# Six feed-forward slots take the quotient from a VectorE reciprocal in place of ScalarE's squared reciprocal root and a refining step

## The chip, the core and the metric

The kernel runs on one core of a Trainium2 chip. The core has five engines with queues of their own: TensorE (PE; its weight loads are PEld), VectorE (DVE), ScalarE (ACT), GpSimd (POOL) and SyncE (SP, which issues all transfers here). Each engine takes its instructions in the order in which they stand in its queue, and waits on semaphores for the others. The metric is the device time of one execution in microseconds: 607.78 us, the median of three runs (607.64 to 608.12).

## The reference

A retention layer is followed by a feed-forward layer with a rational activation. The change lies in the activation, the lines of P, Q and g.

```python
def _attn_ref(q, k, v):                      # B, H, S, D = 4, 8, 768, 64
    for t in range(S):
        state = gamma * state + einsum('bhd,bhe->bhde', k[:, :, t], v[:, :, t])
        y[:, :, t] = scale * einsum('bhd,bhde->bhe', q[:, :, t], state)
    return y

def _moe_ref(x, w_in, w_out, a, b):          # 3072 tokens, 512 -> 2048 -> 512
    h = x @ w_in
    P = a[0] + a[1] * h + a[2] * h * h + a[3] * h * h * h
    Q = 1.0 + abs(b[0]) * abs(h) + abs(b[1]) * h * h
    g = P / (Q + 1e-06)
    return g @ w_out
```

## The kernel before

The 3072 tokens are six blocks of 512, the 2048 hidden columns sixteen tiles of 128. One block with one tile is a slot: 96 of them, numbered by k in the order in which they run. The first two blocks share the first 32 slots by halves; then block 2 has slots 32 to 47, block 3 slots 48 to 63, and so on. Slots 40 to 42 are thus tiles 8 to 10 of block 2, slots 60 to 62 tiles 12 to 14 of block 3. While a block's slots run, the attention work for the next block is put between them.

A slot consists of an input product on TensorE (twelve matmuls at L734, into one of two PSUM banks that the slots use in turn, the tile `ph`), an elementwise chain on a 128x512 tile, and an output product (twelve matmuls at L753, into `po`). TensorE runs the input product of slot k, then the output product of slot k-2, and so on by turns. The input product of slot k+2 needs the bank of slot k, which is free when the last read of `ph` in slot k is over.

The chain of one slot, with the names of its steps:

| step | engine, line | what |
|---|---|---|
| A1 | ACT L796 | q = \|h\| |
| A2 | ACT L805 or POOL L801 | s = \|b0\| + \|b1\| q |
| A3 | ACT L811 | p = a2 + a3 h |
| P1 | POOL L816 | q = q s, so that q + 1 + 1e-6 is the denominator |
| D1 | DVE L824, L825 | p = (p h + a1) h, the numerator without a0 |
| A4 | ACT L831, L832 | s = reciprocal root of the denominator; ph = s squared |
| D2 | DVE L843, L844, L845 | q = denominator times ph; ph = (p + a0) ph; p = (2 - q) ph |
| A6 | ACT L851 | gh = p rounded to the matmul's type |
| P2 | POOL L855 | gl = p - gh |

L843 to L845 refine the estimate of the quotient by one step. The output product takes gh twice and gl once. The tiles p, q and s have two buffers each, gh and gl three.

What runs in which order is fixed beforehand: every step has a number, and the table ORDER lists these numbers; each engine's queue follows from it. In ScalarE's queue slot 40's A6 comes after slot 41's A1 and ahead of its A3 and A2; in the slots without attention work A6 of a slot comes behind A1, A3 and A2 of the next one and ahead of its A4. In VectorE's queue D2 of a slot stands ahead of D1 of the next. The tile qcon holds 1 + 1e-6, and par_sb the four coefficients a and both b. `aside` is false in every slot, as no entry of ENGINES moves that step.

Of the kernel before, what the change touches and what calls it, by code (L numbers as in the profile page):

```python
# [12 lines left out]
AF = mybir.ActivationFunctionType  # L13
ALU = mybir.AluOpType
# [8 lines left out]
class Buffer:  # L23


    def __init__(self, pool, options=None):
        self.pool, self.options, self.banks = pool, options, None
        self.users, self.end = 0, 0


class Step:
    def __init__(self, engines, cost, run, after, rank, takes, uses, tiled):
        self.engines, self.cost, self.run, self.rank = engines, cost, run, rank
        self.takes, self.uses, self.tiled = takes, [*takes, *uses], tiled
        self.after = [(a, 0) if isinstance(a, Step) else a for a in after if a]
        self.start = self.end = self.known = None
        self.waits = 0


class Plan:  # L40
# [7 lines left out]
    def step(  # L48
        self, engines, cost, run, after=(), rank=0.0, takes=(), uses=(), tiled=False, kind=None
    ):  # L50
        self.steps.append(Step(engines, cost, run, after, rank, list(takes), list(uses), tiled))
        return self.steps[-1]
# [12 lines left out]
def tile_retention_rational_ffn(  # L65
# [18 lines left out]
    nc = tc.nc  # L84
# [23 lines left out]
    par_sb = small[:, FEW - 6 : FEW]  # L108
    babs = small[:, FEW : FEW + 2]
    qcon = small[:, FEW + 2 : FEW + 3]  # L110
# [565 lines left out]
    def by(kind, key, default="ACT"):  # L676
        return (ENGINES.get((kind, key), default),)
# [92 lines left out]
    def slot(k, n, f, first, final):  # L770
        cell = {}
        ph = Buffer("psum", lambda: [["b0"], ["b1"]])
        p, q, s, gh, gl = (Buffer(x) for x in ("p", "q", "s", "gh", "gl"))
# [46 lines left out]
        aside = by("N", k, "DVE") == ("POOL",)  # L820
# [7 lines left out]

        def a4(_):
            s_ = cell["s"]  # L830
            nc.scalar.activation(s_, cell["q"], AF.Abs_reciprocal_sqrt, bias=qcon[:, 0:1])  # L831
            nc.scalar.activation(s_ if aside else cell["ph"], s_, AF.Square)  # L832

# [3 lines left out]

        def d2(_):
            p_, q_, ph_ = cell["p"], cell["q"], cell["ph"]
            if aside:  # L840
                nc.vector.scalar_tensor_tensor(ph_, ph_, par_sb[:, 0:1], cell["s"], ALU.add, ALU.mult)
            else:
                nc.vector.scalar_tensor_tensor(q_, q_, qcon[:, 0:1], ph_, ALU.add, ALU.mult)  # L843
                nc.vector.scalar_tensor_tensor(ph_, p_, par_sb[:, 0:1], ph_, ALU.add, ALU.mult)  # L844
            nc.vector.scalar_tensor_tensor(  # L845
                p_, q_, 2.0, ph_, ALU.subtract, ALU.mult, reverse0=True
            )
# [5 lines left out]
        def p2(_):  # L853
# [7 lines left out]
        D1 = step(("DVE",), (1440, 1440), d1, [A3], k, uses=[p, ph], kind="D1")  # L861
        A4 = step(
            ("ACT",), (1265, 1327), a4, [P1, None if aside else D1], k,
            uses=[q, s] if aside else [q, s, ph], kind="A4",
        )
        N1 = aside and step(("POOL",), (1350, 1400), n1, [A4], k, uses=[q, s], kind="N")
        D2 = step(
            ("DVE",), (1370, 1440) if aside else (2030, 2100), d2, [A4, D1, N1], k,
            uses=[p, q, ph, s] if aside else [p, q, ph], kind="D2",
        )  # L870
        A6 = turn("A6", step(("ACT",), (526, 610), a6, [D2], k, [gh], [p], kind="A6"))
        P2 = turn("P2", step(("POOL",), (1253, 1297), p2, [A6], k, [gl], [p, gh], kind="P2"))
# [67 lines left out]
    with tc.manual_schedule(  # L940
# [27 lines left out]
        for k, (n, f) in enumerate(order):  # L968
            while built < NSTEP and starts[built] <= k:
                gate = (gemms_in[k - 1], None) if k else None  # L970
                if built == B:
                    for b in range(0, B, 2):
                        first_states(b, STATES, None)
                many = 2 if built >= PAIRS else 1
                later_chunks(
                    built, many, RANKS.get(built, starts[built] + 0.5), LOADS.get(built, starts[built] / 100),
                    gate,
                )
                built += many
            a, b = turn_of(n, f)  # L980
            first, last = f == a, f + 1 == b
            if last and a:
                load_sums(n, gemms_out[-2])
            slot(k, n, f, first, last)
# [288 lines left out]
```

## Time and profile before

| | |
|---|---|
| median of three runs | 607.78 us |
| the profiled execution | 607.81 us, its span 606.0 us |
| TensorE busy | 98% of the span |
| VectorE busy | 74%, 672 instructions |
| ScalarE busy | 70%, 692 instructions |
| GpSimd busy | 56%, 290 instructions |
| matmuls of input and output product | 390 and 392 ns each in the trace, pipelined: twelve take 2.72 us |
| DVE L843 idle before | 112.1 us in total over 96 slots, 109.1 of it until ACT L832 |

The profile shows one execution. Its span goes from the first to the last instruction; the execution's own time is longer by what lies around the span. A group of instructions has its busy time, the mean duration of one in ns, and the idle time of the engine just ahead of them with what ended it. The timeline gives the start, the duration, the engine, the line and operation, and in brackets the engine's idle time before and what ended it. A duration includes the time until the result has landed, so the next instruction of an engine can begin a little before the end of the one ahead.

### The profile page before, as it was taken

The page shows a single profiled execution, that of the slowest core. Times are in us where ns is not written, and L with a number is a line of the kernel's source. Part 1 is how long each engine was busy: PE and PEld are TensorE (multiplying, and loading weights), DVE is VectorE, ACT ScalarE, POOL GpSimd, SP SyncE. Part 2 cuts the span into 40 slices and gives each one's busy share as a digit, 9 for nine tenths or more (in the row PEclk, how much of TensorE's full clock was granted, in tenths as well). Part 3 has the DMA queues.
Part 4 walks back from the last instruction along what each step waited for, and adds up shares of the span by engine and source line. Part 5 has one row for each costly group of instructions (what it writes and reads, how often), then busy time and mean ns, then how long its engine had stood idle before and what let it go on. Part 6 is the DMA issues. An engine that isn't in the chain of part 4 may idle for free.

```text
span 606.0 us, 12924 instructions
## 1 busy us (share of the span) xinstructions
PE 595.0 (98%) x5228; PEld 485.7 (80%) x5228; DVE 446.7 (74%) x672; ACT 425.7 (70%) x692; POOL 339.9 (56%) x290
## 2 busy tenths in 40 slices
PE   7989999999999999999999999999999999999997
PEld 5757888888888888878888888888888888888885
DVE  5899899998788778666677766567777666666663
ACT  2889799999756575756766765577675676777663
POOL 2789598888747454545435454454363445544452
PEclk9999999999999999999999999999999999999999
DMA  8989506013314253404005101400140000100001
GB/s 310 384 325 415 212 0 210 1 47 107 125 62 159 75 197 91 153 19 157 2 1 174 71 1 37 140 1 18 70 157 2 1 1 1 70 0 1 0 1 70
DMA packets 29980, 58.63 MB, mean 97 GB/s; under 512 B 3168, under 2 KB 8416, under 8 KB 29920
## 3 DMA queue, kind: packets, MB, share of 16 engines
q1 hardware_dynamic: 29920, 57.80, 27.0%
q8 instruction: 41, 0.67, 0.4%
q14 instruction: 19, 0.16, 0.1%
HBM read 49.40 MB, written 8.39 MB: 95 GB/s over the span
## 4 chain that ended last, share of the span: by engine, by line
PE 92%; DVE 1%; ACT 0%; issue 0%
PE po L753 44%; PE ph L734 42%; PE px L279 3%; PE pa L249 2%; PE pk L258 2%; PE po L150 0%; DVE t L706 0%; DVE px L316 0%; DVE u L703 0%; DVE mid L604 0%; DVE p L845 0%; DVE ph L844 0%; DVE state L663 0%; DVE q L843 0%; DVE after L613 0%; DVE p L824 0%
## 5 line engine op out<-in xcount | busy, mean ns | idle before, releaser
L816 POOL TENSOR_TENSOR q<-q,s 128x512 f32<-128x512 f32 x96 | 124.2, 1294 | 173.6 <-ACT s L805 164.2
L734 PE MATMUL ph<-xh,w 128*128 128x512 f32 (+2 forms) x776 | 208.1, 390 | 0.1
L753 PE MATMUL po<-w,gh 128*128 128x512 f32 x768 | 199.8, 392 | 0.0
L734 PEld LDWEIGHTS ph<-xh,w 128*128 128x128 f32 x776 | 143.8, 188 | 30.2 <-DVE p L845 0.5
L753 PEld LDWEIGHTS po<-w,gh 128*128 128x128 f32 x768 | 142.8, 188 | 30.8 <-ACT gh L851 0.3
L843 DVE SCALAR_TENSOR_TENSOR q<-q,small,ph 128x512 f32<-128x512 f32 x96 | 71.7, 747 | 112.1 <-ACT ph L832 109.1
L855 POOL TENSOR_TENSOR gl<-p,gh 128x512 fp32r<-128x512 f32 x96 | 124.3, 1295 | 38.9 <-ACT gh L851 21.9
L831 ACT ACTIVATE s<-q,small 128x512 f32<-128x512 f32 x96 | 69.6, 725 | 64.7 <-POOL q L816 64.7
L753 PE MATMUL po<-w,gl 128*128 128x512 f32 x384 | 110.4, 389 | 0.0
L796 ACT ACTIVATE q<-ph 128x512 f32<-128x512 f32 x96 | 57.3, 597 | 70.4 <-PE ph L734 69.9
L734 PE MATMUL ph<-xl,w 128*128 128x512 f32 (+2 forms) x388 | 103.2, 388 | 0.0
L734 PEld LDWEIGHTS ph<-xl,w 128*128 128x128 f32 x388 | 72.6, 188 | 15.2
L753 PEld LDWEIGHTS po<-w,gl 128*128 128x128 f32 x384 | 72.0, 188 | 15.4 <-POOL gl L855 0.4
L811 ACT ACTIVATE p<-ph,small 128x512 f32<-128x512 f32 x96 | 74.4, 775 | 0.0
L825 DVE SCALAR_TENSOR_TENSOR p<-p,small,ph 128x512 f32<-128x512 f32 x96 | 71.8, 748 | 3.4
L824 DVE TENSOR_TENSOR p<-ph,p 128x512 f32<-128x512 f32 x96 | 65.7, 684 | 8.8 <-ACT p L811 8.4
L844 DVE SCALAR_TENSOR_TENSOR ph<-p,small,ph 128x512 f32<-128x512 f32 x96 | 71.9, 749 | 0.0
L851 ACT CAST gh<-p 128x512 fp32r<-128x512 f32 x96 | 59.2, 616 | 13.2 <-DVE p L845 13.0
L845 DVE SCALAR_TENSOR_TENSOR p<-q,ph 128x512 f32<-128x512 f32 x96 | 65.9, 687 | 3.3
L832 ACT ACTIVATE ph<-s 128x512 f32<-128x512 f32 x96 | 57.8, 602 | 4.2 <-DVE p L825 0.8
L805 ACT ACTIVATE s<-q,small 128x512 f32<-128x512 f32 x73 | 59.3, 813 | 0.1
L715 POOL TENSOR_TENSOR w<-t,w 128x512 fp32r<-128x512 f32 x32 | 41.4, 1298 | 13.8 <-ACT w L712 13.3
(65 smaller groups left out, 429.3 us busy)
## 6 DMA issues: line engine op xcount, KB each, us to landing
v<-in_v SPq DMA_DIRECT2D x34, 256.0 KB, 5.2
raw<-in_w_in SPq DMA_DIRECT2D x16, 512.0 KB, 7.5
raw<-in_w_out SPq DMA_DIRECT2D x16, 512.0 KB, 7.5
qT<-in_qT SPq DMA_DIRECT2D x24, 256.0 KB, 4.6
kT<-in_kT SPq DMA_DIRECT2D x24, 256.0 KB, 4.4
k<-in_k SPq DMA_DIRECT2D x24, 256.0 KB, 4.7
out<-o SPq DMA_DIRECT2D x24, 256.0 KB, 2.4
q2T<-in_q2T SPq DMA_DIRECT2D x10, 256.0 KB, 5.7
```

Source lines behind the costliest of these rows:

```text
L734: nc.tensor.matmul(cell["ph"][:, t0:t1], w[0, f][:, part, kt * P : (kt + 1) * P], x[:, kt, t0:t1], start=(i == 0), stop=(i == 3 * NP - 1),)
L753: nc.tensor.matmul(o_tiles[n][tt], g_[:, tt * P : (tt + 1) * P], w[1, f][:, part], start=(first and m == 0), stop=(last and m == 2),)
L805: nc.scalar.activation(cell["s"], cell["q"], AF.Identity, bias=babs[:, 0:1], scale=babs[:, 1:2])
L811: nc.scalar.activation(cell["p"], cell["ph"], AF.Identity, bias=par_sb[:, 2:3], scale=par_sb[:, 3:4])
L816: nc.gpsimd.tensor_mul(cell["q"], cell["q"], cell["s"])
L824: nc.vector.tensor_mul(p_, ph_, p_)
L825: nc.vector.scalar_tensor_tensor(ph_ if aside else p_, p_, par_sb[:, 1:2], ph_, ALU.add, ALU.mult)
L831: nc.scalar.activation(s_, cell["q"], AF.Abs_reciprocal_sqrt, bias=qcon[:, 0:1])
L843: nc.vector.scalar_tensor_tensor(q_, q_, qcon[:, 0:1], ph_, ALU.add, ALU.mult)
L844: nc.vector.scalar_tensor_tensor(ph_, p_, par_sb[:, 0:1], ph_, ALU.add, ALU.mult)
L845: nc.vector.scalar_tensor_tensor(p_, q_, 2.0, ph_, ALU.subtract, ALU.mult, reverse0=True)
L855: nc.gpsimd.tensor_sub(cell["gl"], cell["p"], cell["gh"].bitcast(F32))
```

## The change

In slots 40, 41, 42, 60, 61 and 62, step A4 is one ScalarE pass that adds 1 + 1e-6 to q and leaves the denominator in s. Step D2 is VectorE's reciprocal of s into the bank `ph`, and one pass p = (p + a0) ph. There is no squaring, and no refining step. All other slots are as before, and ORDER is unchanged. That D2 names s among its tiles has no effect on the order, which is read from the table.

```diff
+DIVIDED = (40, 41, 42, 60, 61, 62)
...
         def a4(_):
             s_ = cell["s"]
+            if k in DIVIDED:
+                nc.scalar.activation(s_, cell["q"], AF.Identity, bias=qcon[:, 0:1])
+                return
             nc.scalar.activation(s_, cell["q"], AF.Abs_reciprocal_sqrt, bias=qcon[:, 0:1])
             nc.scalar.activation(s_ if aside else cell["ph"], s_, AF.Square)
...
         def d2(_):
             p_, q_, ph_ = cell["p"], cell["q"], cell["ph"]
+            if k in DIVIDED:
+                nc.vector.reciprocal(ph_, cell["s"])
+                nc.vector.scalar_tensor_tensor(p_, p_, par_sb[:, 0:1], ph_, ALU.add, ALU.mult)
+                return
             if aside:
...
         D2 = step(
             ("DVE",), (1370, 1440) if aside else (2030, 2100), d2, [A4, D1, N1], k,
-            uses=[p, q, ph, s] if aside else [p, q, ph], kind="D2",
+            uses=[p, q, ph, s], kind="D2",
         )
```

In the changed file the lines up to A4 are numbered 4 higher, those of the refining D2 11 higher. VectorE's queue from slot 40's D2 to slot 41's D2 before (xl and px belong to the attention work between them):

```order
L843 SCALAR_TENSOR_TENSOR q<-q,small,ph 128x512
L844 SCALAR_TENSOR_TENSOR ph<-p,small,ph 128x512
L845 SCALAR_TENSOR_TENSOR p<-q,ph 128x512
L331 TENSOR_TENSOR xl<-px,xh 128x2x2x128 x2
L824 TENSOR_TENSOR p<-ph,p 128x512
L825 SCALAR_TENSOR_TENSOR p<-p,small,ph 128x512
L843 SCALAR_TENSOR_TENSOR q<-q,small,ph 128x512
L844 SCALAR_TENSOR_TENSOR ph<-p,small,ph 128x512
L845 SCALAR_TENSOR_TENSOR p<-q,ph 128x512
```

And the same stretch of VectorE's queue in the changed kernel:

```order
L848 RECIPROCAL ph<-s 128x512
L849 SCALAR_TENSOR_TENSOR p<-p,small,ph 128x512
L335 TENSOR_TENSOR xl<-px,xh 128x2x2x128 x2
L828 TENSOR_TENSOR p<-ph,p 128x512
L829 SCALAR_TENSOR_TENSOR p<-p,small,ph 128x512
L848 RECIPROCAL ph<-s 128x512
L849 SCALAR_TENSOR_TENSOR p<-p,small,ph 128x512
```

Three passes of each slot have become two, and the others keep their places. ScalarE's queue from slot 40's A4 to slot 41's A4 before (xh is attention work):

```order
L831 ACTIVATE s<-q,small 128x512
L832 ACTIVATE ph<-s 128x512
L327 CAST xh<-px 128x2x2x128 x2
L796 ACTIVATE q<-ph 128x512
L851 CAST gh<-p 128x512
L811 ACTIVATE p<-ph,small 128x512
L805 ACTIVATE s<-q,small 128x512
L831 ACTIVATE s<-q,small 128x512
L832 ACTIVATE ph<-s 128x512
```

And in the changed kernel:

```order
L836 ACTIVATE s<-q,small 128x512
L331 CAST xh<-px 128x2x2x128 x2
L800 ACTIVATE q<-ph 128x512
L862 CAST gh<-p 128x512
L815 ACTIVATE p<-ph,small 128x512
L809 ACTIVATE s<-q,small 128x512
L836 ACTIVATE s<-q,small 128x512
```

L836 is the addition in the place of the root, and the squares of L832 are gone; the cast of slot 40 (L862, before L851) still stands ahead of slot 41's A3 and A2.

## The prediction

> **What bounds the kernel now.** I read the head of the page first, then the busy times of the two stretches in which the six slots lie, then the groups, then the timeline engine by engine.
>
> ```profile
> span 606.0 us, 12924 instructions
> ## 1 busy us (share of the span) xinstructions
> PE 595.0 (98%) x5228; PEld 485.7 (80%) x5228; DVE 446.7 (74%) x672; ACT 425.7 (70%) x692; POOL 339.9 (56%) x290
> ```
> ```profile
> 250.00:300.00 50.00, 50.00 (x456) 41.12 (x456) 33.81 (x51) 32.77 (x52) 23.50 (x19) 1.00 0.17 54
> 390.00:416.00 26.00, 26.00 (x117) 21.52 (x116) 16.26 (x24) 17.94 (x30) 12.34 (x10) 1.00 0.00 1
> ```
>
> The columns of the second view are the stretch, its length, the busy time of PE, PEld, DVE, ACT and POOL, the granted clock, and the DMA share. TensorE is busy for 50.00 of 50.00 us around slots 40 to 42 and for 26.00 of 26.00 us around slots 60 to 62, at a clock of 1.00. It waits for nobody there. VectorE (33.81 of 50) and ScalarE (32.77 of 50) have room. Two things follow. Time taken off ScalarE or VectorE in these slots buys nothing by itself: a matmul that never waited cannot wait less. And time added there costs nothing until some matmul's operand or bank comes later than TensorE asks for it. So the question is how much later each slot may give back its bank.
>
> **The change part by part.** Each of the six slots loses one ScalarE pass and two VectorE passes, and gains one reciprocal.
>
> ```profile
> L831 ACT ACTIVATE s<-q,small 128x512 f32<-128x512 f32 x96 | 69.6, 725 | 64.7 <-POOL q L816 64.7
> L805 ACT ACTIVATE s<-q,small 128x512 f32<-128x512 f32 x73 | 59.3, 813 | 0.1
> L851 ACT CAST gh<-p 128x512 fp32r<-128x512 f32 x96 | 59.2, 616 | 13.2 <-DVE p L845 13.0
> L832 ACT ACTIVATE ph<-s 128x512 f32<-128x512 f32 x96 | 57.8, 602 | 4.2 <-DVE p L825 0.8
> ```
> ```profile
> L844 DVE SCALAR_TENSOR_TENSOR ph<-p,small,ph 128x512 f32<-128x512 f32 x96 | 71.9, 749 | 0.0
> L825 DVE SCALAR_TENSOR_TENSOR p<-p,small,ph 128x512 f32<-128x512 f32 x96 | 71.8, 748 | 3.4
> L843 DVE SCALAR_TENSOR_TENSOR q<-q,small,ph 128x512 f32<-128x512 f32 x96 | 71.7, 747 | 112.1 <-ACT ph L832 109.1 <-POOL k L477 2.1 <-POOL w L715 0.8
> L845 DVE SCALAR_TENSOR_TENSOR p<-q,ph 128x512 f32<-128x512 f32 x96 | 65.9, 687 | 3.3
> L824 DVE TENSOR_TENSOR p<-ph,p 128x512 f32<-128x512 f32 x96 | 65.7, 684 | 8.8 <-ACT p L811 8.4
> ...
> L331 DVE TENSOR_TENSOR xl<-px,xh 128x256 fp32r<-128x256 f32 x8 | 2.9, 416 | 0.2 <-ACT xh L327 0.2
> ```
>
> The last two columns before the waits are busy time and mean ns of one. On ScalarE the root of L831 (0.725 us) becomes an addition of the same shape, which I price the same; L805, an addition with a scale too, bounds it at 0.813. The square of L832 (0.602) goes: 6 x 0.60 = 3.6 us less on ScalarE, all of it in time that nobody waits for. The profile shows a single load of ScalarE's tables, at the start:
>
> ```profile
> L121 ACT ACT_TABLE_LOAD x1 | 1.3, 1283 | 0.7 <-PEq L1262 0.7
> ```
>
> So additions and roots already take turns without a load, and dropping the root in six slots neither saves nor adds one. On VectorE three passes of 0.747 + 0.749 + 0.687 = 2.18 us become one reciprocal of unknown length R and one pass of 0.75.
>
> **R is the whole question**, as no reciprocal is in this trace. From below: one ordinary pass, 0.684 (L824). From above I take eight passes: by L824 and L331 a pass costs 0.684 at 512 elements and 0.416 at 256, so 0.536 for the elements and 0.148 fixed, and eight make 0.148 + 8 x 0.536 = 4.44 us. Between ends so far apart I go by the rows that do the same work now. The quotient of a slot is at present a root, a square, a refining pass and a last product: 0.725 + 0.602 + 0.747 + 0.687 = 2.76 us; all five passes that VectorE makes in a slot take 0.684 + 0.748 + 0.747 + 0.749 + 0.687 = 3.62 us. A division made in one instruction, on an engine whose plain pass is a multiplication, I put between these two, at **R = 3.2 us**; this is my choice and not a reading.
>
> [...]
>
> *Term 1, slots 40 and 41.* The timeline of the four engines around slot 40:
>
> ```profile
> 275.45 0.74 DVE L843 SCALAR_TENSOR_TENSOR q<-q,small,ph 128x512 f32<-128x512 f32 x1
> 276.10 0.75 DVE L844 SCALAR_TENSOR_TENSOR ph<-p,small,ph 128x512 f32<-128x512 f32 x1
> 276.89 0.69 DVE L845 SCALAR_TENSOR_TENSOR p<-q,ph 128x512 f32<-128x512 f32 x1
> ...
> 283.16 0.75 DVE L844 SCALAR_TENSOR_TENSOR ph<-p,small,ph 128x512 f32<-128x512 f32 x1
> ```
> ```profile
> 277.63 0.61 ACT L851 CAST gh<-p 128x512 fp32r<-128x512 f32 x1
> 278.14 0.79 ACT L811 ACTIVATE p<-ph,small 128x512 f32<-128x512 f32 x1
> 278.81 0.81 ACT L805 ACTIVATE s<-q,small 128x512 f32<-128x512 f32 x1
> 281.03 0.73 ACT L831 ACTIVATE s<-q,small 128x512 f32<-128x512 f32 x1 [1.41 <-POOL q L816]
> ```
> ```profile
> 279.70 1.29 POOL L816 TENSOR_TENSOR q<-q,s 128x512 f32<-128x512 f32 x1
> ```
> ```profile
> 279.65 1.07 PE L734 MATMUL ph<-xh,w 128*128 128x512 f32 x4
> ...
> 285.09 1.07 PE L734 MATMUL ph<-xh,w 128*128 128x512 f32 x4
> ```
>
> ScalarE's cast of slot 40 (277.63, 0.05 behind the end of L845) stands in its queue ahead of slot 41's L811 and L805, GpSimd's product of slot 41 (279.70) waits for that L805, and slot 41's L831 (281.03) for that product. A late slot 40 therefore makes slot 41 late too, although they share no data. The reciprocal begins where L843 began, at 275.45; 0.04 later comes the last pass (the step from L844's end to L845), 0.75 long, and 0.05 later the cast: at 275.45 + R + 0.84 = 276.29 + R in place of 277.63, so R - 1.34 later. All that hangs on it moves by as much: L831's successor begins at 279.69 + R, takes 0.73, and 0.10 later (see L832 to L843 below) slot 41's reciprocal begins at 280.52 + R. Its bank is free at 280.52 + 2R + 0.84 = 281.36 + 2R. Slot 43's matmuls use that bank (slots alternate between two) and begin at 285.09; now it is free at 283.91 (283.16 + 0.75), 1.18 early. The delay is **2R - 3.73**: nothing below R = 1.87, and at 3.2 it is 2.67 us. Slot 42 at 279.65 needs slot 40's bank, free at 276.29 + R = 279.49: just in time.
>
> *Term 2, slot 42, and term 3, slots 60 to 62.* No attention work lies in this second stretch:
>
> ```profile
> 395.86 0.73 ACT L831 ACTIVATE s<-q,small 128x512 f32<-128x512 f32 x1 [0.23 <-POOL q L816]
> ...
> 401.81 0.72 ACT L831 ACTIVATE s<-q,small 128x512 f32<-128x512 f32 x1 [0.90 <-POOL q L816]
> ```
> ```profile
> 403.27 0.75 DVE L843 SCALAR_TENSOR_TENSOR q<-q,small,ph 128x512 f32<-128x512 f32 x1 [2.06 <-ACT ph L832]
> 403.94 0.75 DVE L844 SCALAR_TENSOR_TENSOR ph<-p,small,ph 128x512 f32<-128x512 f32 x1
> 404.72 0.69 DVE L845 SCALAR_TENSOR_TENSOR p<-q,ph 128x512 f32<-128x512 f32 x1
> 405.33 0.68 DVE L824 TENSOR_TENSOR p<-ph,p 128x512 f32<-128x512 f32 x1
> 406.05 0.75 DVE L825 SCALAR_TENSOR_TENSOR p<-p,small,ph 128x512 f32<-128x512 f32 x1
> ```
> ```profile
> 406.40 1.07 PE L734 MATMUL ph<-xh,w 128*128 128x512 f32 x4
> ```
>
> The steps from one start to the next are 0.67 (L843 to L844, which need not wait for each other), 0.72 (L824 to L825), and 0.79 where a result is waited for (0.75 + 0.04). A slot with a reciprocal thus fills VectorE for R + 0.04 + 0.67 + 0.72 + 0.79 = R + 2.22 us, against 5.44 us of TensorE (279.65 to 285.09). At R = 3.2 that is 5.42: slot 42 costs nothing more. Beyond R = 3.22 each further divided slot adds R - 3.22. For slot 61, the addition ends at 401.81 + 0.72, the reciprocal begins 0.10 later at 402.63 and frees the bank at 402.63 + R + 0.84; slot 63's matmuls ask for it at 406.40. The delay is R - 2.93, at 3.2 **0.27 us**, and slot 62 adds nothing, as slot 42.
>
> The casts and their remainders on GpSimd also come up to 2 us later. They feed the output matmuls of 282.37 and after, which follow one input matmul group later, so they have 2.7 us of cover; GpSimd's scalings of k (L477) behind slot 41's product move with it and are first used slots later; no DMA and no wait of SyncE hangs on these tiles. If ScalarE's addition costs 0.813 instead of 0.725, terms 1 and 3 grow by 0.09 each.
>
> Sum: the profiled execution took 607.81 us (span 606.0 and 1.8 around it), 0.03 above the median of 607.78. 607.81 + 2.67 + 0 + 0.27 = **610.8 us**, 0.5% slower. At R = 2.76 it is 607.81 + 1.79 = 609.6; at R = 3.62, 607.81 + 3.51 + 0.40 + 0.69 + 0.40 = 612.8.
>
> **The rivals.** *One pass.* If the divide streams like any other VectorE operation, R is 0.68, bank 41 is free at 282.7 instead of 283.9, and no matmul notices, as TensorE had no idle time to lose: 607.8 us, not slower. The point from which this decides is R = 1.87, and below 2.47 the loss is within 0.2% (1.2 us, about what a measurement of this kernel can tell from no change). For it speaks that every 512-element pass of VectorE in the groups takes 0.68 to 0.75 whatever it computes, shifts and multiplications alike; against it, that none of them divides. [...]
>
> *Eight passes*, R = 4.44. Term 1 is 2 x 4.44 - 3.73 = 5.15. VectorE's slot of 6.66 us now exceeds TensorE's 5.44 by 1.22, which slot 42 adds. Slot 60's reciprocal begins at 395.86 + 0.73 + 0.10 = 396.69, slot 61's only at 396.69 + 6.66 = 403.35, so bank 61 is free at 408.63, 2.23 late, and slot 62 adds 1.22. 607.81 + 5.15 + 1.22 + 2.23 + 1.22 = 617.6 us. Here VectorE itself becomes the bound of the slots.
>
> *Faster.* It would need a wait of TensorE that ends with these divides. The two stretches show 50.00 of 50.00 and 26.00 of 26.00 us busy, so there is none to shorten.
>
> **How the numbers follow.** R between 2.76 and 3.62, 609.6 to 612.8 us: 0.46, likeliest 610.8. Eight passes, 617.6: 0.27. One pass, 607.8: 0.25. Faster: 0.02. The forecast alone holds less than half, and with the eight passes 0.73, so the range has to take in the one pass as well: 607.5 to 618.0. Slower by over 0.2%: 0.46 + 0.27 = 0.73; within 0.2%: 0.25; faster: 0.02.
>
> **What would show it.** A group of six reciprocals whose mean is R; one about 2.2 us would break the forecast downwards, one over 4 upwards. The root falls to 90 instructions. TensorE should wait once, some 2.7 us, ahead of slot 43's input matmuls, with VectorE's last pass of slot 41 as releaser, and a few tenths ahead of slot 63's. Slot 40's cast should wait for VectorE about 1.9 us with slot 41's ScalarE work queued behind it. If R is right and the wait ahead of slot 43 isn't there, the chain through ScalarE's queue is wrong; if TensorE waits before slot 42, the reciprocal began later than 275.45.

## The result and the profile after

The changed kernel takes **613.37 us** (median of three, 612.5 to 613.72) against 607.78: a ratio of 1.0088, with an interval of 1.0065 to 1.0111. It is slower, inside the range, and 2.6 us above the forecast. The profiled execution is the fastest of the three, 612.5 us. Head of its page and its chain of waits by engine:

```profile
span 610.6 us, 12913 instructions
...
PE 596.4 (98%) x5228; PEld 485.5 (80%) x5228; DVE 458.5 (75%) x666; ACT 422.5 (69%) x686; POOL 339.9 (56%) x290
...
PE 88%; DVE 4%; ACT 1%; POOL 0%; issue 0%; POOLq 0%; DVEq 0%
```

ScalarE does 3.2 us less, VectorE 11.8 us more, and TensorE hardly changes. The groups by line, those of the six slots:

```profile
L838 ACT ACTIVATE s<-q,small 128x512 f32<-128x512 f32 x90 | 65.2, 725 | 58.5 <-POOL q L820 58.5
...
L848 DVE RECIPROCAL ph<-s 128x512 f32<-128x512 f32 x6 | 20.2, 3360 | 1.9 <-ACT s L836 1.6
L849 DVE SCALAR_TENSOR_TENSOR p<-p,small,ph 128x512 f32<-128x512 f32 x6 | 4.5, 748 | 0.2
L836 ACT ACTIVATE s<-q,small 128x512 f32<-128x512 f32 x6 | 4.3, 724 | 3.3 <-POOL q L820 3.3
```

R is 3.36 us. With the last pass that is 4.11 us of VectorE per slot where three passes took 2.18. ScalarE's addition costs what the root cost (0.724 and 0.725). The busy times of the two stretches that were full before, with the same columns as there:

```profile
250.00:300.00 50.00, 47.38 (x443) 38.21 (x442) 38.16 (x45) 28.54 (x45) 22.11 (x18) 1.00 0.17 54
390.00:416.00 26.00, 25.89 (x114) 20.73 (x113) 22.41 (x21) 16.20 (x26) 12.09 (x10) 1.00 0.01 1
```

TensorE now stands still for 2.62 us in the first and 0.11 in the second. The waits between 60 and 606 us name who it waits for (total, times, longest):

```profile
ACT gh L862 <- DVE p L849: 6.7, 6, 2.4
...
PEld ph L738 <- DVE p L849: 4.6, 6, 3.0
...
PE ph L738 <- DVE p L849: 2.6, 1, 2.6
```

The timeline from slot 40's divide to slot 43's matmuls, VectorE, ScalarE, GpSimd and TensorE one after the other:

```profile
275.46 3.35 DVE L848 RECIPROCAL ph<-s 128x512 f32<-128x512 f32 x1
278.85 0.75 DVE L849 SCALAR_TENSOR_TENSOR p<-p,small,ph 128x512 f32<-128x512 f32 x1
...
283.80 3.36 DVE L848 RECIPROCAL ph<-s 128x512 f32<-128x512 f32 x1 [1.29 <-ACT s L836]
287.20 0.75 DVE L849 SCALAR_TENSOR_TENSOR p<-p,small,ph 128x512 f32<-128x512 f32 x1
```
```profile
279.63 0.62 ACT L862 CAST gh<-p 128x512 fp32r<-128x512 f32 x1 [1.88 <-DVE p L849]
280.16 0.77 ACT L815 ACTIVATE p<-ph,small 128x512 f32<-128x512 f32 x1
280.84 0.81 ACT L809 ACTIVATE s<-q,small 128x512 f32<-128x512 f32 x1
283.04 0.72 ACT L836 ACTIVATE s<-q,small 128x512 f32<-128x512 f32 x1 [1.40 <-POOL q L820]
```
```profile
281.72 1.29 POOL L820 TENSOR_TENSOR q<-q,s 128x512 f32<-128x512 f32 x1
```
```profile
284.31 1.07 PE L757 MATMUL po<-w,gl 128*128 128x512 f32 x4
288.00 1.21 PE L738 MATMUL ph<-xh,w 128*128 128x512 f32 x4 [2.62 <-DVE p L849]
...
293.63 1.20 PE L738 MATMUL ph<-xh,w 128*128 128x512 f32 x4
```

Every link of the forecast's chain is there. Slot 40's cast waits 1.88 us with slot 41's L815 and L809 behind it in ScalarE's queue; GpSimd's product and slot 41's reciprocal follow; slot 43's matmuls begin at 288.00 in place of 285.09, on the end of L849 (287.20 + 0.75 = 287.95). The first group of four behind a wait takes 1.21 us and not 1.07. Such a lengthening of 0.1 to 0.2 us, called a refill from here on, comes with each of the six banks that the divides give back (the six waits of PEld above), also where the matmuls themselves begin on time: slot 42's first group takes 1.17 us. The forecast had no refill.

In the rest of this text a shift is how much later a slot's first ScalarE pass (L796 before, L800 after) begins than in the trace of before, less what the shift is at slot 39. It is 3.1 us at slot 43, 3.2 from slot 44 on, 3.3 at slot 62, and 3.9 from slot 64 to the end. The last copy of the output ends 3.7 us later (606.07 against 602.40); the remaining 0.9 of the span's 4.6 lies behind it, in the output's transfers. That tail is 3.6 to 4.6 us long in the thirteen traces of this case. It is 4.5 to 4.6 us in all three traces of the changed kernel, and in two others, those of the copy and of the zeros below; in these five alone an 8 KB packet of the DMA queue that loads instructions starts 1.2 us behind the last copy, among the output's packets, and the last of the output's ends 3.1 to 3.2 us behind that copy, against 2.3 to 2.8 in the other eight. That the packet is the cause, and why it comes in these kernels, no run shows.

This leaves a question that the first trace cannot answer: 3.9 us of delay is not the 5.6 between the medians.

### The profile page after: what moved, and what is told of

Read it like the earlier page. It is cut to its first block, busy times and chain, and to the rows that moved or that the text cites. A ratio compares the mean times of both kernels' runs of the same rounds, so it can differ in the third digit from the quotient of the medians.

```text
span 610.6 us, 12913 instructions
## 1 busy us (share of the span) xinstructions
PE 596.4 (98%) x5228; PEld 485.5 (80%) x5228; DVE 458.5 (75%) x666; ACT 422.5 (69%) x686; POOL 339.9 (56%) x290
## 4 chain that ended last, share of the span: by engine, by line
PE 88%; DVE 4%; ACT 1%; POOL 0%; issue 0%; POOLq 0%; DVEq 0%
PE po L757 41%; PE ph L738 40%; PE px L283 3%; DVE ph L848 2%; PE pa L253 2%; PE pk L262 2%; DVE p L849 0%; PE po L154 0%; DVE px L320 0%; POOL q L820 0%; ACT s L836 0%; DVE t L710 0%; DVE p L828 0%; POOL gl L866 0%; ACT gh L862 0%
## 5 line engine op out<-in xcount | busy, mean ns | idle before, releaser
L854 DVE SCALAR_TENSOR_TENSOR q<-q,small,ph 128x512 f32<-128x512 f32 x90 | 67.2, 746 | 102.6 <-ACT ph L839 101.7
L800 ACT ACTIVATE q<-ph 128x512 f32<-128x512 f32 x96 | 57.3, 597 | 73.7 <-PE ph L738 73.2
L838 ACT ACTIVATE s<-q,small 128x512 f32<-128x512 f32 x90 | 65.2, 725 | 58.5 <-POOL q L820 58.5
L815 ACT ACTIVATE p<-ph,small 128x512 f32<-128x512 f32 x96 | 74.4, 775 | 0.0
L862 ACT CAST gh<-p 128x512 fp32r<-128x512 f32 x96 | 59.2, 617 | 19.4 <-DVE p L856 12.6
L855 DVE SCALAR_TENSOR_TENSOR ph<-p,small,ph 128x512 f32<-128x512 f32 x90 | 67.4, 749 | 0.0
L856 DVE SCALAR_TENSOR_TENSOR p<-q,ph 128x512 f32<-128x512 f32 x90 | 61.8, 687 | 3.1
L809 ACT ACTIVATE s<-q,small 128x512 f32<-128x512 f32 x73 | 59.3, 812 | 0.1
L839 ACT ACTIVATE ph<-s 128x512 f32<-128x512 f32 x90 | 54.2, 602 | 3.8 <-DVE p L829 0.8
```

What stands on the lines that cost most here:

```text
L809: nc.scalar.activation(cell["s"], cell["q"], AF.Identity, bias=babs[:, 0:1], scale=babs[:, 1:2])
L815: nc.scalar.activation(cell["p"], cell["ph"], AF.Identity, bias=par_sb[:, 2:3], scale=par_sb[:, 3:4])
L856: nc.vector.scalar_tensor_tensor(p_, q_, 2.0, ph_, ALU.subtract, ALU.mult, reverse0=True)
```

## The experiments

The kernel before ran beside them on the same chips: medians of 608.16, 607.9 and 607.97 us in three sessions. Ratios are to those.

**A copy in the reciprocal's place.** Does the time come from R alone?

```diff
-                nc.vector.reciprocal(ph_, cell["s"])
+                nc.vector.tensor_copy(ph_, cell["s"])
```

> The six reciprocals are plain copies of s, so these six slots give the numerator times the denominator and no quotient; all else is as in the changed kernel. Theory (the length of the reciprocal, 3.36 us, is the whole loss): the copy takes 0.6 to 0.75 us, TensorE waits nowhere around slots 40 to 45 and 60 to 65, slot 43's input matmuls begin within 0.1 us of where they begin before, 607.8 us. Rival (s held longer, the dropped square, or the other order of waits costs by itself): some of the 3.9 us that the input matmuls come late stays, 609 to 611 us.

Measured: 608.93 us, ratio 1.0014 (1.0005 to 1.0023). The group of the copies:

```profile
L848 DVE COPY ph<-s 128x512 f32<-128x512 f32 x6 | 4.2, 693 | 5.5 <-ACT s L836 5.4
```

With 0.693 us in that place, the shift is 0.00 at every slot from 39 on and TensorE waits for no VectorE pass between 60 and 600 us. So the rest of the change, the missing square and the altered ScalarE queue included, costs and gains nothing; what the change costs is the length of the divide. The median is still 0.8 us above that of the kernel before, against the theory's none. In the profiled execution the last copy ended at 602.11, 0.3 us earlier than before's, and the tail behind it is 0.9 longer, with the packet named above: 0.6 us that no divide makes.

**Slot 40 alone.** Is it ScalarE's queue that hands slot 40's lateness to slot 41, or does each slot only delay its own bank?

```diff
-DIVIDED = (40, 41, 42, 60, 61, 62)
+DIVIDED = (40,)
```

> Slot 40 alone has the reciprocal. Theory (the late cast of slot 40 holds up slot 41's passes in ScalarE's queue, and slot 41's bank is what TensorE waits for): slot 41's divide, with root, square and refining step as before, comes 2.0 us late, its last pass ends at 284.63 + 2.02 instead of 284.63, and slot 43's input matmuls wait 1.5 to 1.6 us; with 0.1 to 0.2 for the refill 609.4 to 609.7 us. Rival (a slot only delays its own bank): slot 40's bank comes just in time for slot 42, no wait over 0.1 us, 607.8 to 608.0 us.

Measured: 609.65 us, ratio 1.0025 (1.0015 to 1.0036), a shift of 1.71. TensorE's row ahead of slot 43:

```profile
287.12 1.20 PE L738 MATMUL ph<-xh,w 128*128 128x512 f32 x4 [1.28 <-DVE p L856]
```

The releaser, what ended the wait, is L856, the last pass of slot 41, a slot that is not divided here and shares no tile with slot 40's quotient. ScalarE's queue hands it on: slot 41's L854 sits idle for 1.99 us until ScalarE's L839 of that slot, so VectorE isn't what holds it. The size follows too: slot 40's cast comes R - 1.34 = 2.02 later; slot 41's bank had been 0.46 early, 1.56 is left, and the refill adds 0.15.

**Slots 40 to 42**, the same constant cut to the first three.

> Slots 40, 41 and 42 have the reciprocal, slots 60 to 62 the old divide. Theory: all that happens before slot 60 stays as in the changed kernel, a wait of 2.6 us ahead of slot 43 and input matmuls 3.2 to 3.3 us late from slot 45 to the end, 611.0 to 611.1 us plus what the tail of the last store adds. Rival (the two groups are alike, each costs half): 2 us late.

Measured: 611.9 us, ratio 1.0075 (1.0061 to 1.0088), with a wait of 2.64 us ahead of slot 43 and a shift of 3.21. Terms 1 and 2 at R = 3.36 give 2.99 + 0.14 = 3.13. The median is 0.8 above the 611.0 to 611.1 of the theory. The five executions stand in two groups, 611.5 to 611.9 and twice 613.2; the two have the lower mean clocks, 0.996 and 0.997 against 0.998 and 0.999. The delay does not explain that.

**The cast later.** Slot 40's A6 and P2 (steps 899, 900) moved behind slot 41's A3, A2 and P1 in the order, so that slot 41 no longer waits for slot 40's divide in ScalarE's queue (the piece of ORDER that changes):

```diff
-903, 888, 996, 899, 890, 905, 900, 904, 907, 987, 913, 906, 908
+903, 888, 996, 890, 905, 904, 907, 987, 913, 906, 899, 900, 908
```

> All six slots as changed, but slot 40's cast and remainder stand behind slot 41's passes in the queues of ScalarE and GpSimd. Theory (half of the first wait comes through these queues): slot 41's addition stays where it is before, at 281.0, its reciprocal begins when VectorE is through with slot 41's numerator, at 282.3 instead of 283.8; the wait ahead of slot 43 falls from 2.6 to 1.2 us and the input matmuls at the end come 2.4 to 2.5 us late instead of 3.9, 610.2 to 610.4 us. Rival (VectorE alone sets the pace, the queue order doesn't matter): 3.9 us late as in the changed kernel.

Measured: 610.75 us, ratio 1.0046 (1.0034 to 1.0059). The same row of TensorE:

```profile
286.86 1.21 PE L738 MATMUL ph<-xh,w 128*128 128x512 f32 x4 [1.09 <-DVE p L849]
```

The wait falls from 2.62 to 1.09 us with nothing changed but the place of one cast and its remainder; the shift is 1.69 behind slot 43 and 2.43 at the end. More than half of the wait was the queue. What is left of it is VectorE's own pace. The median is 0.35 above the theory's range; in the profiled execution the opening, all that lies ahead of slot 40, took 0.4 us longer than before.

**Slots 60 to 62 alone**, the same constant cut to the last three.

> Slots 60, 61 and 62 have the reciprocal, slots 40 to 42 the old divide. Theory: what the changed kernel loses behind slot 60 stays alone, 0.35 to 0.45 us ahead of slot 63 and 0.15 to 0.2 us ahead of slot 64 with the refills, 0.7 us in the start of all later input matmuls; 0.7 us over the kernel before. Rival (the second loss exists only because the first has shifted the work): 0.0 us.

Measured: 609.22 us, ratio 1.0023 (1.0013 to 1.0034), a shift of 0.71. Term 3 and the pace of slot 62 at R = 3.36 give 0.43 + 0.14 = 0.57; refills make up the rest. The median is 1.3 us above that of the kernel before and not 0.7: in the profiled execution the opening is 0.5 us longer and the tail 0.5 us, so the shift is the firmer number here.

**Six other slots**, chosen where the bank comes free well ahead of the matmuls that use it: `DIVIDED = (33, 46, 54, 56, 60, 70)`.

> Again six slots with the reciprocal, but slots 33, 46, 54, 56, 60 and 70, each behind or beside attention matmuls that keep TensorE from asking for the bank so early, and no two next to each other. Theory (the 3.36 us cost nothing where the bank, and what is queued behind the divide, have room): the reciprocals take 3.36 us as ever, VectorE is busy some 12 us longer than before, and no input matmul comes more than 0.1 us late; within 0.2% of the kernel before. Rival (six long reciprocals cost their 1.2 to 2 us of extra VectorE time somewhere in any case): 2 us or more.

Measured: 608.13 us, ratio 1.0007 (0.9999 to 1.0016), no difference that shows. Its group of reciprocals:

```profile
L848 DVE RECIPROCAL ph<-s 128x512 f32<-128x512 f32 x6 | 20.2, 3361 | 4.1 <-ACT s L836 4.0
```

Six reciprocals of the same 3.36 us, 11.4 us more of VectorE, and a shift of 0.10 at most (behind slot 60). The divides are not dear in themselves; they are dear where neighbours in one queue have no slack.

**Two halves.** The reciprocal in two pieces of 256 columns, to see what of it goes by the element:

```diff
-                nc.vector.reciprocal(ph_, cell["s"])
+                for x in (slice(0, TB // 2), slice(TB // 2, TB)):
+                    nc.vector.reciprocal(ph_[:, x], cell["s"][:, x])
```

> Each reciprocal is made in two halves of 128x256. Theory (the time goes by elements, about six passes' worth: (3.36 - 0.15) / 512 each): one half takes 1.7 to 1.8 us, both 3.5 to 3.6, and the input matmuls at the end come 4.2 to 5.0 us late instead of 3.9. Rival (a fixed start-up of the divide makes most of it): a half takes 2.4 us or more, and the loss is above 8 us.

Measured once: 613.81 us. The group:

```profile
L849 DVE RECIPROCAL ph<-s 128x256 f32<-128x256 f32 x12 | 21.1, 1760 | 1.9 <-ACT s L836 1.3
```

1.760 us for 256 columns and 3.360 for 512: 6.25 ns an element ((3.360 - 1.760) / 256) and 0.16 us fixed, so cutting it in two adds 0.16 a slot and no more. The shift, though, was 5.0 at slot 43 and 6.1 at the end, more than any theory had said, as TensorE's clock was 0.50 behind the wait, from 288.9 to 292.3. That opened the second question.

**The changed kernel again**, to see whether that was the halves' doing.

> The changed kernel as it is, beside the kernel before on the same chip. Theory: its input matmuls come 3.9 us late as in its first trace, and the rest of the first comparison (5.6 us by the medians) is the time between the last copy and the end, which differs from run to run by about 1 us whatever the kernel: 3.7 to 4.9 us over the kernel before. Rival (the change makes TensorE's clock fall): 5.6 us again, with a clock below 1 in the middle of the span.

Measured: 613.51 us (612.68 to 615.09), ratio 1.0098 (1.0081 to 1.0115). What was put there as the rival is what the trace shows. TensorE around slot 43, then the busy times with the granted clock (third column from the end):

```profile
287.72 1.92 PE L738 MATMUL ph<-xh,w 128*128 128x512 f32 x4 [2.60 <-DVE p L849]
289.44 1.91 PE L738 MATMUL ph<-xl,w 128*128 128x512 f32 x4
291.15 1.18 PE L738 MATMUL ph<-xh,w 128*128 128x512 f32 x4
```
```profile
287.00:288.00 1.00, 0.28 (x1) 0.28 (x2) 1.00 (x2) 0.30 (x1) 0.00 (x0) 0.97 0.00 0
288.00:289.00 1.00, 1.00 (x3) 0.72 (x3) 0.96 (x2) 0.94 (x2) 0.60 (x1) 0.50 0.00 0
...
291.00:292.00 1.00, 1.00 (x5) 0.77 (x5) 1.00 (x1) 0.00 (x0) 0.00 (x0) 0.83 0.00 0
```

The wait is the 2.6 us of the first trace, and no matmul waits longer. But from 287.9 to 291.3 the clock is 0.50, two groups take 1.9 us instead of 1.1, and the shift behind slot 43 is 4.6 and not 3.2. The first trace of this very kernel has 1.00 throughout. So the low clock came in one of these two traces and not in the other.

**Zeros in the gap, a longer gap, and the change a third time**, on one chip. The zeros are eight matmuls into the open output bank ahead of slot 43's input product (step 924):

```diff
-    11: 3, 14: 3, 24: 12, 53: 4, 250: 2, 266: 3, 267: 3, 272: 3, 291: 10, 362: 3,
+    11: 3, 14: 3, 24: 12, 53: 4, 250: 2, 266: 3, 267: 3, 272: 3, 291: 10, 362: 3, 924: 8,
```

> The changed kernel with eight matmuls of zeros added into the open output bank just ahead of slot 43's input product, in the time in which TensorE waits for VectorE (13 such matmuls take 3.2 us in the trace of before, so eight some 1.9 us). They compute nothing and TensorE reaches them at about 285.1, while slot 41's last pass frees the bank at about 287.9. Theory (the 2.6 us gap makes the granted clock fall in some executions, and that is the second part of the loss): with a gap of some 0.8 us left, the clock stays at 1.00 from 284 to 296, no matmul group takes 1.9 us, slot 44 and later start 3.2 to 3.4 us later than before in the profile and the end 3.9, and the time is 611.6 to 612.6, about 1 us below the changed kernel of the same call, with a narrower spread. Rival A (the low clock has nothing to do with the gap): the clock falls as often as without the zeros, and the time is that of the changed kernel. Rival B (the zeros delay TensorE): the input product starts later than 288.0 and the time is up to 1.9 us above the changed kernel's faster executions.

The longer gap:

```diff
-                nc.vector.reciprocal(ph_, cell["s"])
+                for _ in range(2 if k == 41 else 1):
+                    nc.vector.reciprocal(ph_, cell["s"])
```

> The changed kernel with slot 41's reciprocal issued twice (the second overwrites the first with the same values), so that the wait ahead of slot 43 grows from 2.6 to about 6.0 us and nothing else changes. Theory of the clock: a gap this long makes the granted clock fall to 0.50 in every execution, so that the time is that of the changed kernel's best executions (612.5) plus 3.36 for the second reciprocal plus about 1.6 for the slow stretch, 617.0 to 618.0, with the 0.50 seen in the windows behind slot 43's start. Rival (the clock falls by chance, not by the gap): 612.5 to 613.5 plus 3.36, so 615.9 to 616.9, and a clock of 1.00 there in the profile as likely as not.

And the change itself:

> The changed kernel once more, beside the kernel with the zeros on the same chip. Theory of the clock: times between 612.3 and 615.1 in two groups, median 613 to 613.6, and a profile that shows either a clock of 1.00 with slot 44 starting 3.2 us later than before, or 0.50 for some 3.4 us with slot 44 starting 4.6 us later. Rival: every execution alike within 0.3 us.

The change for the third time: 613.57 us (612.23 to 614.71), ratio 1.0088 (1.0074 to 1.0103). The shift behind slot 43 is 4.6 again, with these rows of TensorE and clock:

```profile
287.66 1.32 PE L738 MATMUL ph<-xh,w 128*128 128x512 f32 x4 [2.61 <-DVE p L849]
288.78 1.91 PE L738 MATMUL ph<-xl,w 128*128 128x512 f32 x4
```
```profile
288.00:289.00 1.00, 1.00 (x5) 0.81 (x4) 0.96 (x2) 0.89 (x2) 0.66 (x1) 0.79 0.00 0
289.00:290.00 1.00, 1.00 (x3) 0.78 (x3) 0.91 (x1) 0.00 (x0) 0.63 (x1) 0.50 0.00 0
...
292.00:293.00 1.00, 1.00 (x5) 0.82 (x5) 0.96 (x2) 0.70 (x2) 0.00 (x0) 1.00 0.00 0
```

Here the clock falls 0.9 us after the matmuls have begun again. By their times alone the six executions spread over 2.5 us without two clear groups, so that part of the expectation did not come. With the mean clock beside the time, the fifteen executions of the change in three sessions do part: the ten with a mean clock of 0.996 or less took 613.37 to 615.09 us, the five above it 612.23 to 612.97. None of the 47 executions of the kernel before, beside the experiments, is under 0.997. A mean clock does not say where in the span the clock was low.

The zeros: TensorE and the clock.

```profile
286.76 1.90 PE L154 MATMUL po<-zeros 128*128 128x512 bf16 x8
289.52 1.20 PE L738 MATMUL ph<-xh,w 128*128 128x512 f32 x4 [0.86 <-DVE p L849]
290.56 1.07 PE L738 MATMUL ph<-xl,w 128*128 128x512 f32 x4
```
```profile
284.00:300.00 16.00, 15.13 (x66) 11.21 (x65) 13.44 (x13) 9.51 (x15) 7.67 (x7) 1.00 0.02 8
...
14.00:16.00 2.00, 2.00 (x48) 1.76 (x44) 1.58 (x4) 0.34 (x2) 0.00 (x0) 0.50 1.06 405
```

The gap is 0.86 us, the clock stays at 1.00, no group takes 1.9, and the shift is 3.2 behind slot 43 and 3.9 at the end: as in the first trace, 1.4 us less than in the second and third. The zeros delay nothing. But the time is 613.1 us (611.53 to 614.03), ratio 1.0073 (1.0059 to 1.0087), only 0.5 below the change beside it and above the 611.6 to 612.6 expected. In the profiled execution, the slowest of the six, the second row shows why: the clock was 0.50 for some 3.4 us near 15 us, in the opening, where nothing was edited, and every slot from 0 on is 1.5 us later. None of the other twelve traces has that stretch. One trace with a clock of 1.00 behind slot 43 would show little, as the change without zeros has such a trace too. The five other executions with the zeros have mean clocks of 0.997 to 1.000, where ten of the change's fifteen have 0.996 or less; that speaks for the zeros. The times don't separate the gain from the spread that every kernel has.

The longer gap: 616.88 us (616.78 to 617.21), ratio 1.0144 (1.0131 to 1.0158).

```profile
291.51 2.08 PE L738 MATMUL ph<-xh,w 128*128 128x512 f32 x4 [6.00 <-DVE p L850]
293.39 1.91 PE L738 MATMUL ph<-xl,w 128*128 128x512 f32 x4
```
```profile
288.50:288.60 0.10, 0.00 (x0) 0.00 (x0) 0.10 (x1) 0.00 (x0) 0.00 (x0) 0.76 0.00 0
288.60:288.70 0.10, 0.00 (x0) 0.00 (x0) 0.10 (x1) 0.00 (x0) 0.00 (x0) 0.50 0.00 0
295.30:295.40 0.10, 0.10 (x1) 0.10 (x1) 0.10 (x1) 0.00 (x0) 0.00 (x0) 0.61 0.00 0
295.40:295.50 0.10, 0.10 (x2) 0.07 (x2) 0.10 (x1) 0.00 (x0) 0.00 (x0) 1.00 0.00 0
```

A wait of 6.00 us, and a clock of 0.50 from 288.55 to 295.38. The shift at slot 43 is 8.21: the 3.2 of the first trace, 3.36 for the second reciprocal, and 1.6 for the clock. The time lies 0.1 below what the theory said and at the upper edge of what the rival said, so it does not decide; the clock in the trace does for that execution, and the mean clocks of all four, 0.992 or 0.993, and their times within 0.43 us speak for the same in the others. The theory's number started from 612.5, an execution with a long tail.

## Why the prediction was right, and what it lacked

**TensorE is the bound, ScalarE's saving is worth nothing.** Right: with a short pass in the divide's place nothing moves, though a square per slot is gone.

**R.** Bounds 0.684 and 4.44, chosen 3.2, measured 3.36: between the two sums of rows (2.76 and 3.62) that it was put between, and past both thresholds, 1.87 and 3.22. That it came so close is luck: no row of the trace before ties the divide's length to the passes that it replaces, and the prediction called 3.2 a choice. The range of 607.5 to 618.0 took in the one pass and the eight as well, so to lie in it says little of the mechanism; the waits below do. The eight passes of the upper bound were the author's choice, and no run shows such a count: by the element, the measured 6.25 ns are six times the 0.536 / 512 = 1.05 ns that the prediction's rows give an ordinary pass, as an estimate from these two numbers.

**Term 1, through ScalarE's queue.** Right in mechanism and releaser (one wait, slot 41's last pass, 1.88 us at the cast), and both halves of it were shown: slot 40 alone delays slot 43, and moving the cast takes 1.5 us off the wait. At R = 3.36 the formula 2R - 3.73 gives 2.99, and slot 43's matmuls begin 2.91 later. One statement on the way was wrong: bank 41 was not free at 283.91, 1.18 early. L845 reads `ph` too:

```profile
283.94 0.69 DVE L845 SCALAR_TENSOR_TENSOR p<-q,ph 128x512 f32<-128x512 f32 x1
```

It ended at 284.63, 0.46 early. The sum did not use that slack, so it stands; but with slot 40 alone the slack counts, and the 1.71 of that run fits 0.46 and not 1.18.

**Terms 2 and 3.** At the measured R the formulas give R - 3.22 = 0.14 at slot 42 and again at 62, and R - 2.93 = 0.43 at slot 61, together 0.71 where 0.27 was forecast, because R was 0.16 longer. The rows of TensorE in the sixties:

```profile
404.21 1.16 PE L738 MATMUL ph<-xh,w 128*128 128x512 f32 x4
...
410.02 1.20 PE L738 MATMUL ph<-xh,w 128*128 128x512 f32 x4
...
415.65 1.20 PE L738 MATMUL ph<-xh,w 128*128 128x512 f32 x4
```

Slot 63's matmuls began at 406.40 before and slot 64's at 411.84: they are 3.62 and 3.81 later, after 3.25 at slot 62 (400.96 to 404.21). Slot 61's divide thus added 0.37 and slot 62's 0.19, with the refill of the slot ahead in each. Slot 42's added 0.19 (slot 44's matmuls began at 290.53 before and at 293.63 now, 3.10 later after 2.91). The formulas held to 0.06.

**Tables and covers.** No second load of ScalarE's tables; the casts and remainders had the cover that was claimed, as no matmul waits for either.

**The sum.** With the measured R the same working gives 607.81 + 2.99 + 0.14 + 0.43 + 0.14 = 611.5 us, against 610.8 forecast: 0.7 of the miss of 2.6 is the size of R. The refills make 0.2 (3.9 of delay against 3.7). Two terms the sum lacked altogether. One is the clock: 1.4 us, in two of three profiled executions of the change. The two unprofiled ones of the first comparison, 613.37 and 613.72, have a mean clock of 0.995, as those two have, and the profiled one of 612.5 has 1.000; that their clock fell behind slot 43 too is likely, but was not seen. The other is the end: in all three traces of the change the last copy comes 0.3 us earlier than the shift says, and the tail is 0.9 longer than before's, so 0.6 more. Together 607.8 + 3.9 + 1.4 + 0.6 = 613.7; the last 0.3 to the median is what the opening varies by, which took 0.3 us less in the second and third trace than before. The prediction read "clock 1.00" as a property of the stretch; it was measured with TensorE busy for 50.00 of 50.00 us, and behind a wait of 2.6 us it held in one trace of the change in three.

**The rivals.** One pass: out, as the copy shows what it would have given. Eight passes: out by R, 3.36 us and not 4.44. Faster: no wait was there to shorten, and none was.

## What to carry to other kernels

Where TensorE was never idle, as here, passes taken off another engine paid nothing (six squares of 0.60 us less on ScalarE, and a shift of 0.00 with the copy), and the price of a longer one was set by who stood behind it in each queue: six divides cost 0.1 us of delay in slots with slack and 3.9 us as two runs of neighbours. Before a step is lengthened, look in the queue of the next engine for work of another slot that stands behind it; moving one cast was worth 1.5 us here. And a wait of TensorE of 2.6 us cost half as much again in clock (1.4 us) in two traces of three, so such a gap is worth breaking up: waits of 1.3, 1.1 and 0.9 us left the clock at 1.00, in one trace each. Filled with zeros it left the clock at 1.00 in the one trace taken, but a gain in time was not shown.

## What the runs showed of the hardware

The reciprocal on VectorE takes 3.36 us for 128x512 in fp32 and 1.76 for 128x256, the same to 0.01 us in all slots.

TensorE's clock fell to 0.50 around a gap of 2.6 us in two traces of the change and around one of 2.8 with the halves, and did not in the first trace of the change nor with slots 40 to 42 alone, both with the same 2.6 us; gaps of 1.3, 1.1 and 0.9 us left it at 1.00, in one trace each. The low stretch lasted 3.4 us wherever the gap was short (287.9 to 291.3 in the second trace) and 6.83 us (288.55 to 295.38), twice that, behind the gap of 6.0. It began 0.2 us after the matmuls had resumed in the second trace, 0.9 after in the third, and before that with the long gap. How the clock is set, no run shows.

One length comes back in the traces' records of the clock: half of 6.83 is 3.41 us, and the record at 1.00 is 604.16 us long in the first trace of the change and 600.75 in that of the kernel before, 3.41 apart. As an estimate from these lengths, a trace can be divided into steps of 3.41 us, counted from where its clock changes: from the start of the low stretch, or, where none lies behind slot 43, from the end of the record at 1.00 (610.45 in the first trace) or from the end of the low stretch in the opening (16.6 with the zeros). The gap can then be laid against the steps. TensorE's busy time is the number behind the length. The first trace of the change, the second, and the third:

```profile
282.77:286.18 3.41, 2.60 (x12) 1.83 (x10) 2.38 (x1) 2.58 (x4) 2.73 (x4) 1.00 0.00 0
286.18:289.60 3.42, 1.60 (x7) 1.32 (x8) 3.25 (x5) 1.25 (x2) 1.70 (x2) 1.00 0.00 0
```
```profile
284.52:287.94 3.42, 0.82 (x4) 0.40 (x3) 3.38 (x3) 1.06 (x3) 1.48 (x2) 1.00 0.00 0
```
```profile
285.16:288.58 3.42, 0.92 (x4) 0.79 (x5) 3.35 (x4) 1.06 (x3) 1.50 (x2) 1.00 0.00 0
```

In the first trace a border of two steps cut the gap in two, 2.60 and 1.60 us of work were left in the two steps, and the clock stayed at 1.00; with slots 40 to 42 alone it was 2.58 and 1.62, with the zeros in the gap 2.56 in its one step, and it stayed too. In the other two the gap lay in one step, but for 0.1 us in the third trace, with 0.82 and 0.92 us of work left, and the next step had 0.50; the halves had 0.62 and the long gap 0.37 and 0.45, each with 0.50 behind it. So by this estimate the same gap of 2.6 us cost clock or not by where a border fell. Between 0.92 and 1.60 us of work nothing was seen here, and in the opening of the zeros' trace a step with 1.80 us of other, much shorter matmuls was followed by 0.50 as well. No run moved the gap against the steps on purpose, so that the work left in a step decides was not shown.
